# Feed-forward layers by seven block products in place of eight, in a four-layer attention and feed-forward kernel

## The chip, the cores and the metric

The kernel runs on one core of a Trainium2 chip. The metric is the device time of one execution, in microseconds (us). The engines are named as in the profile: PE is the tensor engine and PEld its weight loads, DVE is VectorE, ACT is ScalarE, POOL is GpSimd, and SP issues the DMA transfers. Code and diffs are cuts: several lines of the kernel may stand on one line, and "..." marks what is left out.

## The reference, cut to what matters

There are four layers on 2048 tokens of width 1024: linear attention (A), feed-forward (B), A, B. Each has a layer norm ahead of it and a residual sum behind it.

```python
def _A_ref(x, wqkv, wo):            # 32 heads of 32
    ...
    pq, pk = phi(q), phi(k)         # phi(t) = where(t > 0, t + 1, exp(t)) + 1e-6
    kv  = einsum("bhsd,bhse->bhde", pk, v);  z = sum over s of pk
    o   = einsum(pq, kv) / (einsum(pq, z) + 1e-6)
    return o @ wo
def _B_ref(x, w_gate, w_up, w_down):      # D = 1024, F = 3584
    return ((x @ w_gate) * (x @ w_up)) @ w_down
x = x + _A_ref(_layernorm(x), ...); x = x + _B_ref(_layernorm(x), ...)   # twice
```

## The kernel before

A small planner records each operation with the memory that it reads and writes, and derives the semaphore waits. Each engine has its own list, taken in order.

The feed-forward layer walks 4 blocks of 512 tokens. For each block it makes 28 gate and 28 up chains of eight matmuls (L756), multiplies them, and then runs the down product over 28 tiles (L776):

```python
for m, bank in ((0, b_g), (1, b_u)):
    ... [e.matmul(psb(bank), wgu[:, w, m, k, cc:cc + 128], xnT[:, k, sb * 512:(sb + 1) * 512],
                  start=(k == 0), stop=(k == KT - 1)) for k in range(KT)]          # L756
P.add("act", lambda e: e.copy(gsb[gi], psb(b_g)), ...)                             # L761
P.add("dve", lambda e: e.tensor_tensor(out=hT[:, hs, :], in0=psb(b_u), in1=gsb[gi], op=ALU.mult), ...)
```

In attention, three stretches follow each other: the K and Q projections; the stretch that forms the K·V products; and the output stretch. The division by the denominator ("normalisation" below, `norm`) runs per token tile of 128 tokens. Eleven of the 16 tiles are normalised during the K·V stretch, the other five inside the output stretch, all through one product buffer:

```python
NNORM = 11
def norm(i):
    P.add("dve", ... tensor_tensor(out=pbuf, in0=x_res[:, i, :], in1=zb, op=ALU.mult))   # L588
    ... tensor_reduce(out=den, in_=pbuf ...); + 1e-6; reciprocal                          # DVE
    P.add("pool", ... tensor_tensor(out=asb[b], in0=pbuf, in1=rden (broadcast), op=ALU.mult))  # L597
    P.add("sp", ... dma_start_transpose(xnT[:, :, i * 128:(i + 1) * 128], asb[b]))
...
for i in range(NST):                     # the output stretch
    if na[0] < NST and i % 3 == 0:
        norm(na[0]); na[0] += 1
    nxt.step_t(1); nxt.b1_one()          # layer norm of the next layer: transpose, scale factor
    y_grp(i, 0)                          # 8 matmuls (L714), residual added on DVE (L720)
    nxt.b2_one()                         # layer norm applied, on ACT (L406)
    y_grp(i, 1)                          # 8 matmuls, copied by ACT (L723), added on POOL (L724)
    if i >= 1:
        nxt.start(i - 1)                 # statistics on DVE (L389), 1/sqrt on POOL (L392, L394)
```

## Time and profile before

The median is 1697.24 us (1696.1 to 1698.99, 4 runs). The first view is the head of the page: busy time, share of the span and instruction count of each engine, and then the chain of work that ended last, by line.

```profile
PE 1636.5 (97%) x7577; PEld 740.3 (44%) x7662; DVE 596.8 (35%) x978; ACT 385.7 (23%) x609; POOL 235.2 (14%) x271
...
PE ps L756 46%; PE ps L776 23%; PE ps L569 7%; POOL arena L597 3%; DVE arena L528 2%; DMA arena<-arena 2%; POOL arena L724 1%; PE ps L634 1%; DVE arena L526 1%; DVE arena L389 1%; POOL arena L394 1%; POOL arena L392 1%; ACT arena L406 1%; SPq L600 1%; ACT arena L723 1%
```

PE is the limit: it is nearly always busy, and two lines of the feed-forward layers make up 69% of the chain. The second view holds groups of instructions: line, engine, operation, shapes, count, then total busy us and mean ns of one, then the idle time before them and what ended it.

```profile
L756 PE MATMUL ps<-arena 128*128 128x512 f16 x3584 | 775.1, 379 | 0.0
...
L714 PE MATMUL ps<-arena 128*128 128x512 bf16 x502 | 122.2, 397 | 34.0 <-DVE arena L720 21.0
```

A matmul lasts 379 ns, but matmuls overlap: 775.1 us over 3584 is 216 ns each, and that is the cost of one more. The output stretch (L714) is another matter: PE idles 34 us before its matmuls, waiting for evacuations.

The third view is the table of stretches, cut at the first matmul of each part: start and end, length, busy us (and instructions) of each engine, granted PE clock (1.00 is full rate), DMA share, GB/s. In order: K/Q, K·V, output, feed-forward, and the same again.

```profile
core 0: us, PE busy (x) PEld busy (x) DVE busy (x) ACT busy (x) POOL busy (x), PEclk, DMA share, GB/s
0.00:124.40 124.40, 111.99 (x528) 50.25 (x539) 97.27 (x181) 79.64 (x125) 51.38 (x79) 1.00 0.39 116
124.40:199.20 74.80, 71.20 (x372) 33.99 (x379) 42.10 (x62) 22.55 (x37) 22.33 (x12) 0.98 0.45 103
199.20:277.70 78.50, 60.42 (x253) 24.58 (x257) 49.66 (x90) 22.98 (x29) 39.05 (x45) 0.96 0.49 102
277.70:858.00 580.30, 579.25 (x2670) 262.86 (x2689) 134.48 (x217) 71.23 (x118) 16.69 (x39) 1.00 0.49 137
858.00:961.60 103.60, 103.07 (x472) 46.98 (x481) 75.39 (x123) 72.63 (x118) 39.56 (x34) 1.00 0.30 89
961.60:1034.90 73.30, 69.76 (x373) 33.59 (x379) 42.01 (x62) 22.44 (x37) 22.25 (x12) 1.00 0.39 91
1034.90:1112.20 77.30, 61.40 (x252) 25.30 (x256) 49.65 (x90) 22.99 (x29) 38.98 (x45) 0.93 0.53 115
1112.20:1695.50 583.30, 579.43 (x2669) 262.73 (x2687) 106.23 (x159) 71.24 (x118) 4.93 (x9) 1.00 0.41 118
```

The feed-forward layers are full (PE busy 579 of 580 and 583 us). The two output stretches are not: PE is busy 60 of 78.5 us and 61 of 77.3 us, so they hold 34 us of idle PE between them.

### The profile page before, as it was taken

Reading aid. Unit: us, or ns where it says so; the run is one execution under the profiler, and the core shown is the slowest. Engines: PE = TensorE matmul, PEld = TensorE weight load, DVE = VectorE, ACT = ScalarE, POOL = GpSimd, SP = SyncE. Lnnn points to the kernel's source line nnn. Section 1 sums busy time; section 2 is a strip of 40 time slices with the busy share of each in tenths; the row PEclk is TensorE's granted clock in tenths of the full one; section 3 lists DMA queues with packets and bytes.
Section 4 is the critical chain, followed back from the end, with each engine's and each line's share of the span. In section 5 each row is a group of like instructions: output and inputs, shape, how many; then the busy total and the mean of one; then the engine's idle time right before and its main releaser. Section 6 shows DMA issues by size and latency. Waiting matters only on the chain.

```text
span 1695.5 us, 18381 instructions
## 1 busy us (share of the span) xinstructions
PE 1636.5 (97%) x7577; PEld 740.3 (44%) x7662; DVE 596.8 (35%) x978; ACT 385.7 (23%) x609; POOL 235.2 (14%) x271
## 2 busy tenths in 40 slices
PE   8999978999999999999999998799999999999999
PEld 3444423444444444444444443244444444444444
DVE  6885665112211211221257667641112111211211
ACT  6661323110110011011057523231101101100110
POOL 4442353000000000000033234520000000000000
PEclk9999999999999999999999999999999999999999
DMA  5143635952453355253460146379405513531520
GB/s 199 38 122 76 151 72 119 320 162 61 131 153 101 106 149 149 57 155 112 138 204 1 51 100 148 74 190 282 128 26 157 152 51 108 149 106 46 156 68 22
DMA packets 370692, 203.07 MB, mean 120 GB/s; under 512 B 101168, under 2 KB 351280, under 8 KB 370608
## 3 DMA queue, kind: packets, MB, share of 16 engines
q1 hardware_dynamic: 370608, 201.89, 43.6%
q8 instruction: 61, 1.00, 0.2%
q14 instruction: 23, 0.19, 0.0%
HBM read 165.68 MB, written 12.58 MB: 105 GB/s over the span
## 4 chain that ended last, share of the span: by engine, by line
PE 77%; issue 7%; POOL 7%; DVE 5%; ACT 2%; DMA 2%; SPq 1%; POOLq 0%; ACTq 0%
PE ps L756 46%; PE ps L776 23%; PE ps L569 7%; POOL arena L597 3%; DVE arena L528 2%; DMA arena<-arena 2%; POOL arena L724 1%; PE ps L634 1%; DVE arena L526 1%; DVE arena L389 1%; POOL arena L394 1%; POOL arena L392 1%; ACT arena L406 1%; SPq L600 1%; ACT arena L723 1%
## 5 line engine op out<-in xcount | busy, mean ns | idle before, releaser
L756 PE MATMUL ps<-arena 128*128 128x512 f16 x3584 | 775.1, 379 | 0.0
L756 PEld LDWEIGHTS ps<-arena 128*128 128x128 bf16 x3584 | 350.3, 98 | 423.5 <-ACT arena L761 1.5
L776 PE MATMUL ps<-arena 128*128 128x512 bf16 x1752 | 384.7, 379 | 2.1
L762 DVE TENSOR_TENSOR arena<-ps,arena 128x512 bf16<-128x512 f32 x224 | 155.1, 692 | 595.5 <-PE ps L756 591.3
L761 ACT CAST arena<-ps 128x512 bf16<-128x512 f32 x224 | 131.2, 587 | 907.8 <-PE ps L756 907.8
L776 PEld LDWEIGHTS ps<-arena 128*128 128x128 bf16 x1792 | 175.4, 98 | 211.4
L569 PE MATMUL ps<-arena 128*128 128x512 bf16 x1003 | 224.4, 380 | 6.8 <-DVE arena L528 4.6
L787 DVE TENSOR_TENSOR arena<-ps,arena 128x512 bf16<-128x512 f32 x64 | 44.3, 692 | 318.0 <-PE ps L776 318.0
L714 PE MATMUL ps<-arena 128*128 128x512 bf16 x502 | 122.2, 397 | 34.0 <-DVE arena L720 21.0
L569 PEld LDWEIGHTS ps<-arena 128*128 128x128 f16 x1024 | 99.1, 98 | 127.6 <-DVE arena L528 9.1
L634 PE MATMUL ps<-arena 128*128 128x512 bf16 x499 | 114.1, 379 | 0.6
L524 ACT ACTIVATE arena<-ps 128x512 f32<-128x512 f32 x128 | 76.6, 598 | 120.9 <-PE ps L569 91.6
L392 POOL TENSOR_SCALAR arena<-arena 128x1 f32<-128x1 f32 x64 | 22.0, 343 | 574.4 <-DVE arena L391 574.3
L714 PEld LDWEIGHTS ps<-arena 128*128 128x128 f16 x512 | 49.9, 102 | 105.9 <-DVE arena L720 30.9
L389 DVE BATCH_NORM_STATS2 arena<-arena 128x6 f32<-128x512 bf16 x128 | 88.3, 690 | 9.4 <-DMA arena<-in_A_x_dram 4.3
L581 POOL TENSOR_TENSOR arena<-arena 128x512 f32<-128x512 f32 x60 | 74.9, 1251 | 111.5 <-DVE arena L528 111.5
L528 DVE SCALAR_TENSOR_TENSOR arena<-ps,arena 128x512 bf16<-128x512 f32 x128 | 88.5, 692 | 4.4
L525 ACT ACTIVATE arena<-arena 128x512 f32<-128x512 f32 x128 | 81.0, 633 | 4.1
L597 POOL TENSOR_TENSOR arena<-arena 128x1024 f16<-128x1024 f32 x32 | 61.3, 1915 | 124.6 <-DVE arena L595 114.9
L526 DVE TENSOR_SCALAR arena<-arena 128x512 f32<-128x512 f32 x128 | 66.4, 519 | 33.1 <-ACT arena L525 32.1
L634 PEld LDWEIGHTS ps<-arena 128*128 128x128 f16 x512 | 49.3, 98 | 55.7
L406 ACT ACTIVATE arena<-arena 128x1024 f16<-128x1024 bf16 x32 | 39.8, 1243 | 111.0 <-DVE arena L400 70.1
(41 smaller groups left out, 361.1 us busy)
## 6 DMA issues: line engine op xcount, KB each, us to landing
arena<-in_B_w_gate_dram SPq DMA_DIRECT2D x112, 512.0 KB, 3.8
arena<-in_B_w_up_dram SPq DMA_DIRECT2D x112, 512.0 KB, 4.8
arena<-in_B_w_down_dram SPq DMA_DIRECT2D x14, 1024.0 KB, 10.1
arena<-in_A_wqkv_dram SPq DMA_DIRECT2D x12, 1024.0 KB, 7.9
arena<-in_A_x_dram SPq DMA_DIRECT2D x31, 256.0 KB, 5.3
arena<-in_A_wo_dram SPq DMA_DIRECT2D x4, 1024.0 KB, 5.8
x_scratch<-arena SPq DMA_DIRECT2D x16, 256.0 KB, 2.0
xn_scratch<-arena SPq DMA_DIRECT2D x16, 256.0 KB, 2.4
```

The lines of the kernel that those rows point to most:

```text
L389: P.add("dve", (lambda h: lambda e: e.bn_stats(st[j][:, 6 * h:6 * h + 6], x_res[:, i, (D // 2) * h:(D // 2) * (h + 1)]))(h), rd=r_x(i, (D ...
L525: P.add("act", lambda e: e.activation(etmp[r], etmp[r], AF.Exp, scale=-1.0), rd=er, wr=er)
L526: P.add("dve", lambda e: e.tensor_scalar(out=etmp[r], in0=etmp[r], scalar1=1e-6, scalar2=None, op0=ALU.add), rd=er, wr=er)
L528: P.add("dve", lambda e: e.scalar_tensor_tensor(out=dst_ap, in0=psb(bank), scalar=C1, in1=etmp[r], op0=ALU.add, op1=ALU.max), prd=[bank], ...
L569: return [e.matmul(psb(bank), xnT[:, k, i * 128:(i + 1) * 128], w[:, k, h * 512:(h + 1) * 512], start=(k == 0), stop=(k == KT - 1)) for k ...
L597: P.add("pool", lambda e: e.tensor_tensor(out=asb[b].rearrange("p (h c) -> p h c", c=32), in0=pbuf.rearrange("p (h c) -> p h c", c=32), in ...
L634: return [e.matmul(psb(bank), xr[:, t, j * 128:(j + 1) * 128], pk[:, h, t, :], start=(t == 0), stop=(t == NST - 1)) for t in range(NST)]
L714: return [e.matmul(psb(bank), xnT[:, g, i * 128:(i + 1) * 128], wp[:, g, dh * 512:(dh + 1) * 512], start=(g == 0), stop=(g == NG - 1)) for ...
L756: return [e.matmul(psb(bank), wgu[:, w, m, k, cc:cc + 128], xnT[:, k, sb * 512:(sb + 1) * 512], start=(k == 0), stop=(k == KT - 1)) for k ...
L761: P.add("act", lambda e: e.copy(gsb[gi], psb(b_g)), prd=[b_g], wr=R(O_GS[gi], 1024))
L762: P.add("dve", lambda e: e.tensor_tensor(out=hT[:, hs, :], in0=psb(b_u), in1=gsb[gi], op=ALU.mult), prd=[b_u], rd=R(O_GS[gi], 1024), wr=R( ...
L776: r.append(e.matmul(psb(bank), hT[:, hs, st_ * 128:(st_ + 1) * 128], wd[:, ft, dh * 512:(dh + 1) * 512], start=(ft == 0), stop=(ft == NFT ...
```

## The change

The intent: a product of matrices cut into 2 by 2 blocks can be formed with seven block products and some additions, in place of eight products. The change does this one level deep. Gate and up are cut by contraction half and output half, the tokens in pairs of 512. The kernel now makes two passes of 1024 tokens per layer; a pass has 28 units (gate and up alternating) of seven products of four matmuls, and a down part of seven products. One bank of PSUM (the memory that matmuls write to), X, is a running chain: product 1, then 6, then 7, then 4 are added into it, and ACT copies the partial sum out between them.

```diff
+def unit(ps_, u):                       # one gate or up block: 7 products of 4 matmuls (L878)
+    X, Y, Z = B_GX[u % 2], B_GY[u % 2], B_GZ
+    # 1: a11 b11   2: a12 b21   3: S4 b22   4: a22 T4   5: S1 T1   6: S2 T2   7: S3 T3
+    part1:   pe("1", X, True);  cp(0, X);  pe("2", Z, True);  fin(0, Z, 0)
+    part2:   pe("6", X, False); cp(1, X)                       # cp = ACT copy of the bank (L882)
+    part3:   pe("5", Y, True);  pe("7", X, False); cp(2, X); fin(1, Y, 2)
+    part_p4: pe("4", X, False); fin(2, X, None)                # one unit later
+    part_p3: pe("3", Y, False); fin(3, Y, 1)                   # fin = DVE, bank + copy (L602)
+def prep_s(n):                          # weight sums S1..S4, DVE, 16-bit (L599); first pass only
+    tt(sv[:, 0], a21, a22, ALU.add); tt(sv[:, 1], sv[:, 0], a11, ALU.subtract); ...
+def wd_tick(ph):                        # sums of the down weights, spread over the first pass
+    if ph == 0: wd_load(j)
+    elif ph == 1: wd_prep(j); wd_store(j); wdn[0] += 1
 ...
+cur[0](); prev[1](); cur[2](); prev[3](); ring_issue(); cur[4]()
+if jit: store_s(n); prep_s(n + 2)       # jit = first pass of the first feed-forward layer
+ticks(u)                                # layer norm steps, down-weight sums
```

The weight sums go to DRAM as they are made and are streamed back in the three later passes. Sums of activations (T1 to T4) and of the hidden blocks are made on DVE too. The activation and the hidden operands are fp16.

The same diff also touches attention:

```diff
-    NNORM = 11
+    NNORM = 14
-    pbuf = vf(O_P, D)
+    pbufs = [vf(o, D) for o in O_P]     # O_P = [O_ZACC, RE], used as pbufs[i % 2]
-    if na[0] < NST and i % 3 == 0:
+    if na[0] < NST:
         norm(...)
     nxt.step_t(1); nxt.b1_one()
+    if i >= 2:
+        nxt.start(i - 2)
     y_grp(i, 0); nxt.b2_one(); y_grp(i, 1)
-    if i >= 1:
-        nxt.start(i - 1)
```

Besides, the second attention layer takes its tokens in the order in which the new down part finishes them. PSUM banks and SBUF places are reassigned.

## The prediction

> **What bounds the kernel now.** The tensor engine. The page has PE busy 97% of 1695.5 us at a granted clock of 0.994. In the chain of waits, the gate/up line (L756) and the down line (L776) hold 46% and 23%. The table of stretches gives the two feed-forward layers 582 and 585 us, PE busy 581 in each; they run 5376 matmuls of 512 columns at 216 ns (775.1 us over 3584). PE idles mainly in the attention output stretches (204 to 276 us: busy 53.5 of 71.6; 1042 to 1110: 52.7 of 68.5). There the waits view has PE waiting for evacuations (L720, L723), which sit behind the normalisation chain: one product buffer, 5.1 us a step.
>
> **Removed.** One matmul in eight: 5376 becomes 4704. 672 x 0.216 = 145 us, all on the critical path. Operand types should not change the rate: fp16 activations with bf16 weights already run at 216 ns.
>
> **Added, mostly off the path.**
> - VectorE: 536 PSUM evacuations at 0.692 us (L762's duration) for 288; about 336 SBUF additions or products of 512 16-bit elements, 64 of 1792, 16 of 2048. The trace has no such operation. [...]
> - ScalarE: 392 PSUM copies at 0.59 us for 224, about +100 us.
> - A gate and up pair costs PE 56 x 0.216 = 12.1 us; [...]ScalarE 4.1. A copy has two or three products (0.86 us each) to finish. Hidden.
> - Exception: the first pass of the first feed-forward layer, where the weight sums are made[...]. [...]two of the down-weight preparations are queued directly behind their own load. I expect PE to wait there about 16 us (10 to 35), little in later passes.
> - DMA grows from 202 to about 250 MB. The heaviest stretch asks about 275 GB/s; a slice of the present page moves 320 GB/s without PE waiting.
> - Starts of passes and layers, longer lead into the first pass: +8 us.
>
> **Moved.** The normalisation gets two product buffers and 14 tokens (was 11) during the previous stretch, so the output stretches should shrink from 72 and 68 to about 60 us: -20 us.
>
> **Sum.** 1697 - 145 + 16 + 8 - 20 is about 1556 us. Range 1532 to 1595. Faster by over 2%: 0.96; within 2%: 0.03; slower: 0.01.
>
> **What would show it right or wrong.** Matmul groups: 3136 gate/up and 1568 down matmuls, 216 ns each by busy time over count. Stretches: feed-forward layers near 530 (first) and 512 us (second), PE busy about 508 in each; PE's missing time concentrated in the first layer's first pass, released by VectorE. [...] Attention output stretches near 60 us each.
>
> **What would make it wrong.** [...]VectorE held up in order behind loads or layer norm, so that PE stalls on PSUM banks in every pass; the single bank for the second product turning into a per-unit wait; no gain in the attention stretches (1575 us).

The sum came to about 1556 us: 1697 - 145 + 16 + 8 - 20. The 16 us, and the 8 us for starts, are estimates.

## The result, and the profile after

The changed kernel takes 1547.34 us (1544.87 to 1547.89, 4 runs). The ratio to the kernel before is 0.9113, with a 95% interval of 0.9097 to 0.9129. Ratios here are the mean time of one kernel's fast runs over that of the other's fast runs of the same rounds, so they differ a little from the ratio of the medians. All outputs are right. The head of the page after, and its groups:

```profile
PE 1492.5 (97%) x6925; PEld 674.1 (44%) x6990; DVE 967.5 (63%) x1642; ACT 503.3 (33%) x793; POOL 246.6 (16%) x271
```

```profile
L878 PE MATMUL ps<-arena 128*128 128x512 f16 x3136 | 685.4, 381 | 17.5 <-ACT arena L882 12.3 <-DVE arena L602 5.2
...
L882 ACT ACTIVATE arena<-ps 128x512 f32<-128x512 f32 x336 | 200.4, 596 | 551.4 <-PE ps L878 550.6 <-DVE arena L602 0.8
...
L599 DVE TENSOR_TENSOR arena<-arena 128x512 f16<-128x512 bf16 x140 | 53.1, 419 | 10.4 <-DMA arena<-in_B_w_down_dram 9.9
...
L599 DVE TENSOR_TENSOR arena<-arena 128x2048 f16<-128x2048 f16 x16 | 19.5, 1216 | 0.0
```

PE is as full as before, with less to do. The 16-bit additions of 512 elements take 419 ns where a bf16 pair is written as fp16 (x140, above), and 429 ns where all is fp16 (x196). DVE has 371 us more work. The table of stretches after, in the same order:

```profile
0.00:124.10 124.10, 111.77 (x529) 50.02 (x540) 97.28 (x181) 79.48 (x125) 51.48 (x79) 1.00 0.40 117
124.10:198.30 74.20, 71.21 (x372) 34.04 (x379) 56.48 (x74) 22.31 (x37) 37.35 (x15) 0.98 0.51 114
198.30:256.00 57.70, 55.28 (x252) 24.84 (x256) 46.56 (x91) 24.86 (x30) 31.99 (x45) 1.00 0.56 116
256.00:784.20 528.20, 514.10 (x2343) 230.04 (x2352) 328.91 (x605) 131.39 (x210) 11.10 (x27) 0.99 0.67 205
784.20:901.00 116.80, 107.07 (x472) 47.41 (x480) 79.03 (x139) 77.31 (x124) 42.50 (x43) 0.97 0.40 116
901.00:972.90 71.90, 69.54 (x371) 33.61 (x378) 55.61 (x73) 22.19 (x37) 37.36 (x15) 1.00 0.56 121
972.90:1030.70 57.80, 55.38 (x253) 24.88 (x256) 45.35 (x88) 25.01 (x31) 32.02 (x45) 1.00 0.66 162
1030.70:1546.20 515.50, 508.14 (x2343) 229.28 (x2351) 258.28 (x397) 120.77 (x200) 2.74 (x5) 1.00 0.53 164
```

Line by line against the table before, the two feed-forward layers give 52.1 and 67.8 us, together 119.9. The two output stretches give 20.8 and 19.5, together 40.3. The K·V stretches give 2.0, the first K/Q stretch 0.3. The second K/Q stretch **costs** 13.2 us. The sum is 149.3, the difference of the two spans (1695.5 and 1546.2).

Two things stand out: over a quarter of the gain (40.3 of 149.3 us) comes from the output stretches of attention, and one stretch got worse. A third shows when the feed-forward layers are cut into passes. These are the four gate/up passes:

```profile
256.00:445.20 189.20, 176.27 (x786) 77.01 (x786) 142.37 (x314) 62.26 (x102) 2.96 (x5) 0.97 0.75 237
...
529.60:699.80 170.20, 169.50 (x785) 76.50 (x785) 95.86 (x171) 66.66 (x106) 6.33 (x16) 1.00 0.74 207
...
1030.70:1204.10 173.40, 170.09 (x786) 76.32 (x786) 87.15 (x148) 62.25 (x102) 2.74 (x5) 1.00 0.56 167
...
1288.50:1458.80 170.30, 169.56 (x786) 76.57 (x786) 84.54 (x140) 58.51 (x98) 0.00 (x0) 1.00 0.58 177
```

784 matmuls at 216 ns are 169.3 us. Three passes are within about 4 us of that; the first loses 20. DVE is busy only 142 of its 189 us, so DVE is not full there. What PE waited for in the first pass stands at the end of its group:

```profile
L878 PE MATMUL ps<-arena 128*128 128x512 f16 x784 | 176.2, 387 | 12.9 <-ACT arena L882 7.7 <-DVE arena L602 5.2
```

### The profile page after: what moved, and what is told of

The parts are those of the page before. It is cut to its first block, busy times and chain, and to the rows that moved or that the text cites. A ratio compares the mean times of both kernels' runs of the same rounds, so it can differ in the third digit from the quotient of the medians.

```text
span 1546.2 us, 18008 instructions
## 1 busy us (share of the span) xinstructions
PE 1492.5 (97%) x6925; PEld 674.1 (44%) x6990; DVE 967.5 (63%) x1642; ACT 503.3 (33%) x793; POOL 246.6 (16%) x271
## 4 chain that ended last, share of the span: by engine, by line
PE 79%; DVE 11%; issue 4%; ACT 3%; POOL 2%; DMA 1%; SPq 0%; DVEq 0%; POOLq 0%; ACTq 0%
PE ps L878 41%; PE ps L988 22%; PE ps L807 6%; PE ps L661 5%; PE ps L727 4%; DVE arena L550 3%; DVE arena L548 2%; DVE arena L408 1%; DVE arena L681 1%; DVE arena L684 1%; DMA arena<-in_B_w_down_dram 1%; DVE arena L599 1%; ACT arena L425 1%; POOL arena L413 1%; ACT arena L882 1%
## 5 line engine op out<-in xcount | busy, mean ns | idle before, releaser
L878 PE MATMUL ps<-arena 128*128 128x512 f16 x3136 | 685.4, 381 | 17.5 <-ACT arena L882 12.3
L602 DVE SCALAR_TENSOR_TENSOR arena<-ps,arena 128x512 f16<-128x512 f32 (+2 forms) x536 | 365.0, 689 | 437.3 <-PE ps L988 160.8
L878 PEld LDWEIGHTS ps<-arena 128*128 128x128 f16 (+1 forms) x3136 | 306.0, 98 | 396.3 <-ACT arena L882 21.4
L882 ACT ACTIVATE arena<-ps 128x512 f32<-128x512 f32 x336 | 200.4, 596 | 551.4 <-PE ps L878 550.6
L988 PE MATMUL ps<-arena 128*128 128x512 f16 (+1 forms) x1548 | 337.4, 379 | 1.1
L661 PE MATMUL ps<-arena 128*128 128x512 bf16 x1003 | 228.3, 384 | 16.0 <-DVE arena L550 13.9
L988 PEld LDWEIGHTS ps<-arena 128*128 128x128 f16 x1568 | 153.4, 98 | 185.0
L599 DVE TENSOR_TENSOR arena<-arena 128x512 f16<-128x512 f16 (+3 forms) x416 | 222.6, 556 | 17.0 <-DMA arena<-in_B_w_down_dram 9.9
L661 PEld LDWEIGHTS ps<-arena 128*128 128x128 f16 x1024 | 99.6, 99 | 140.3 <-DVE arena L550 20.3
L807 PE MATMUL ps<-arena 128*128 128x512 bf16 x502 | 111.0, 379 | 4.8 <-DVE arena L813 3.9
L727 PE MATMUL ps<-arena 128*128 128x512 bf16 x499 | 114.2, 379 | 0.6
L425 ACT ACTIVATE arena<-arena 128x1024 f16<-128x1024 bf16 x48 | 59.5, 1239 | 132.2 <-DVE arena L419 119.7
L546 ACT ACTIVATE arena<-ps 128x512 f32<-128x512 f32 x128 | 76.0, 594 | 64.3 <-PE ps L661 37.9
L690 POOL TENSOR_TENSOR arena<-arena 128x1024 f16<-128x1024 f32 x32 | 80.0, 2499 | 89.2 <-DVE arena L688 88.0
L807 PEld LDWEIGHTS ps<-arena 128*128 128x128 f16 x512 | 49.8, 98 | 65.8 <-DVE arena L813 4.9
L727 PEld LDWEIGHTS ps<-arena 128*128 128x128 f16 x512 | 49.2, 98 | 55.7
```

What stands on the lines that cost most here:

```text
L599: P.add("dve", lambda e: e.tensor_tensor(out=out, in0=a, in1=b, op=op), rd=rd, wr=wr, prd=prd)
L602: P.add("dve", lambda e: e.scalar_tensor_tensor(out=out, in0=a, scalar=sc, in1=b, op0=ALU.mult, op1=op1), rd=rd, wr=wr, prd=prd)
L661: return [e.matmul(psb(bank), xnT[:, k, i * 128:(i + 1) * 128], w[:, k, h * 512:(h + 1) * 512], start=(k == 0), stop=(k == KT - 1)) for k ...
L727: return [e.matmul(psb(bank), xr[:, t, j * 128:(j + 1) * 128], pk[:, h, t, :], start=(t == 0), stop=(t == NST - 1)) for t in range(NST)]
L807: return [e.matmul(psb(bank), xnT[:, g, i * 128:(i + 1) * 128], wp[:, g, dh * 512:(dh + 1) * 512], start=(g == 0), stop=(g == NG - 1)) for ...
L878: P.add("pe", lambda e: [e.matmul(psb(bank), w[:, k, :], x[:, k, :], start=(start and k == 0), stop=(k == 3), skip_group_check=True) for k ...
```

## The experiments

Ten kernels were run, in three groups. Each group shares its runs of the kernel before, whose medians were 1697.21, 1697.49 and 1696.31 us. The changed kernel was not run again in them, so a difference from its 1547.34 us is one between groups.

### Why the first pass loses 20 us, and the second K/Q stretch 13 us

The PE timeline at the start of the first pass shows the pattern (start, length, instructions; in brackets the idle time before and what ended it):

```profile
256.02 7.07 PE L878 MATMUL ps<-arena 128*128 128x512 f16 x32
265.26 7.90 PE L878 MATMUL ps<-arena 128*128 128x512 f16 x28 [2.17 <-ACT arena L882]
275.79 7.90 PE L878 MATMUL ps<-arena 128*128 128x512 f16 x28 [2.63 <-ACT arena L882]
285.86 4.67 PE L878 MATMUL ps<-arena 128*128 128x512 f16 x13 [2.17 <-ACT arena L882]
```

PE stops three times for an ACT copy. And the 28 matmuls after the first two stops take 7.9 us each, where the same 28 take 6.2 us in run `e2_wd_early` below at full rate: the records of the granted clock show a half-rate period of 3.41 us after each of the three stops (the first from about 266.4 us). So each of the first two costs its idle time and, on top, 1.7 us (7.9 less 6.2); for the third, with as long a period, the same is our estimate. The 12.9 us of idle and three times 1.7 us make 18 of the 20 us. The chain that ended last says what the copy waited for:

```profile
272.76 1.10 DVE arena L599 x3
273.86 0.14 DVE arena L419
274.02 1.24 ACT arena L425
275.26 0.49 ACT arena L882
275.79 5.33 PE ps L878 x16
```

Read upwards: PE waits for a 0.6 us copy (L882); the copy stands behind a layer norm application on ACT (L425, 1.24 us); that waits for a scale factor of 0.2 us on DVE (L419); and that stands behind the weight sums (L599). Later in the pass, three stops have another cause:

```profile
311.11 5.64 DMA arena<-in_B_w_down_dram
...
316.77 0.44 DVE arena L599
...
318.33 0.61 DVE arena L602
318.99 29.54 PE ps L878 x136
```

Here a sum of down weights waits on DVE for its own load, issued just before it, and the evacuation for which PE waits (L602) stands behind. These three stops (2.50, 0.80 and 1.93 us) were not followed by half rate: the granted clock stayed at 1.00 from 290.3 us to the end of the pass. In the second K/Q stretch the chain runs in a ring of 9.9 us per token tile, and again L419 and L425 are links of it:

```profile
851.73 0.70 DVE arena L408
...
853.06 0.58 POOL arena L413
...
853.66 0.23 DVE arena L419
853.91 1.24 ACT arena L425
855.15 0.49 ACT arena L546
```

L546 is the first step of the K/Q evacuation. The rival to all this "in-order" theory: these stretches simply hold more work than DVE and ACT can do, and its order does not matter. Three single edits tell the two apart, each alone, and then all together.

**Layer norms of the second K/Q stretch on DVE, as before the change.**

```diff
     lnp.on_act = False
+    if not is_last:
+        nxt.on_act = False
```

> The changed kernel, with the layer norms of the second K/Q stretch (784 to 901 us, 116.8 us) applied on VectorE as the kernel before does, not on ScalarE. Theory A: PE stalls there because the ScalarE normalisation (1.24 us, L425) waits in order for a VectorE statistic and holds back the K/Q evacuation on ScalarE; taking it off ScalarE brings the stretch to 104 to 109 us and the time down by 8 to 13 us. Rival B: the stretch is longer because five more tokens are normalised inside it at all (statistics and normalisation work moved in from the feed-forward layer); then the engine that does it matters little and the stretch stays within 3 us of 116.8.

Measured: 1537.96 us (1535.62 to 1540.43, 4 runs), ratio 0.906. The stretch fell to 105.6 us. ACT no longer waits for L419 at all, and DVE has more work in the stretch than it had (81.0 us against 79.0), ACT 4 us less (73.4 against 77.3). Neither more tokens in the stretch nor the work on DVE was therefore what made it long; the ACT link was. Theory A holds. The 2 us that remain against the kernel before (103.6) were not followed up.

**Down-weight loads issued one block ahead.**

```diff
-if ph == 0 and j < NJ: wd_load(j)
-elif ph == 1 and j < NJ: wd_prep(j); wd_store(j); wdn[0] += 1
+if ph == 0 and j == 0: wd_load(0)
+elif ph == 1 and j < NJ:
+    wd_prep(j); wd_store(j)
+    if j + 1 < NJ: wd_load(j + 1)
+    wdn[0] += 1
```

> The changed kernel, with each down-weight load issued directly after the sums of the block before it, so that a load never has its own sums queued right behind it. Theory A: the three stops of PE at 311, 353 and 387 us in the first pass of the first feed-forward layer (three waits of VectorE for that load, 5.3 to 5.8 us each in the chain, 9.9 us of VectorE idle in all) go; the first pass falls from 188.9 us by 4 to 10 us and the total by as much. Rival B: VectorE is simply full in that pass (142 us busy of 189, but little room left per unit), so the work is only moved and the pass changes by less than 2 us.

Measured: 1541.74 us (1540.7 to 1543.2, 4 runs), ratio 0.9083. The first pass fell from 189.2 to 183.7 us. VectorE still waits for the load, but 5.0 us in place of 9.9, at most 1.8 us at a time, and PE waits for L602 once, 1.5 us, in place of three times, 5.2 us. Theory A holds, at the lower end, and not all of the 5.5 us is the loads': the first stop of the pass, again of 2.17 us, was this time not followed by half rate (the 28 matmuls after it took 6.22 us, against 7.90), which is worth 1.7 us.

**The layer norm application always uses a scale factor made a unit earlier.**

```diff
 self.step_t(1)
-if self.q_n: self.b2_one(); self.b1_one()
-else:        self.b1_one(); self.b2_one()
+self.b2_one(); self.b1_one()
```

> The changed kernel, where a unit's ScalarE normalisation always uses a statistic made a unit earlier (one order of two calls changed). Theory A: the stalls in the first three or four units of the first pass (256 to 290 us: 33 us for about 20.9 us of matmuls, granted clock 0.80 to 0.85) come from ScalarE, which stands in order behind that statistic, which stands in order behind four weight sums on VectorE; the stalls go, the first pass shrinks by 7 to 12 us, the second layer's first pass by 1 to 3 us. Rival B: VectorE's load of weight sums and statistics itself is too much in these units, and the stalls stay within 3 us of what they are.

Measured: 1533.67 us (1531.41 to 1537.28, 5 runs), ratio 0.9041. The first pass fell to 180.4 us and the second layer's first pass from 173.4 to 170.3. The first 37 us of the pass now ran at a granted clock of 1.00 where the changed kernel had 0.85 in its first 34 us. No work was removed; two calls changed places. Theory A holds. The execution profiled is the fastest of the five, and 3.0 us of its gain lie in the first K·V stretch (71.2 us against 74.2), which the edit doesn't touch: there a stop that was 2.57 us is 1.21 us, and the four matmuls after it take 1.04 us, where they took 1.89.

**All three.**

> All three edits in one kernel. If the three are separate causes their gains add: about 1547 less 25 to 30 us, near 1520 us. If the stalls hide each other (VectorE full in the first pass), the sum falls short of the parts by over 5 us.

Measured: 1520.92 us (1520.22 to 1521.05, 4 runs), ratio 0.8959 to the kernel before. The three gains by medians, 9.4, 5.6 and 13.7 us, add to 28.7; together they give 26.4. So they are nearly separate causes, as far as such sums can tell: the mean granted clock of the executions profiled was 0.993 in the changed kernel, 0.993, 0.994 and 0.998 with one edit each, and 0.999 with all three, so fewer half-rate periods are part of the last two gains. This is the fastest kernel. Its first pass and its second K/Q stretch:

```profile
256.20:432.50 176.30, 170.63 (x785) 75.95 (x785) 141.94 (x314) 62.36 (x102) 2.95 (x5) 1.00 0.84 254
...
771.60:877.20 105.60, 103.78 (x472) 46.57 (x480) 80.94 (x139) 73.35 (x119) 42.24 (x43) 1.00 0.43 120
```

DVE does the same 142 us of work in this pass as before the repair, in 13 us less time. That settles that the pass was not short of DVE throughput. Seven of its 176 us are still above the matmuls' own 169.3.

### Where the 40 us in the output stretches come from

The diff changes three things there: two product buffers, 14 tiles normalised ahead, and the layer norm statistics of a tile started one tile later. It also uses other PSUM banks. The first three were put one after another into the kernel **before**, with no block product anywhere.

**Two buffers and 14 tiles ahead** (`NNORM = 14`, `pbufs[i % 2]`, `norm` at every step of the output stretch until all are done):

> The kernel before, with nothing of the seven products: only two product buffers for the attention normalisation, and 14 of its 16 tokens done in the stretch ahead (was 11). Theory A: this alone is what shortens the attention output stretches from 71.6 and 68.5 us to about 52; the kernel before gains 28 to 36 us, to 1661 to 1669 us. Rival B: the later start of the layer norms in that stretch, their other order and the other PSUM banks do it, and this part alone gains under 12 us.

Measured: 1669.64 us (1668.17 to 1670.04, 4 runs), ratio 0.9838. The output stretches fell from 78.5 and 77.3 to 65.7 us each. The gain of 27.9 us is just short of what theory A said, and the stretches did not reach the 57.8 us of the changed kernel. So it is most of the cause, not all.

The product on GpSimd itself became longer: 1915 ns on average with one buffer in the kernel before, where VectorE waits for it (39.3 us in all), and 2471 ns with two. In the changed kernel, also with two, it takes 2499 ns on average: 26 of the 32 overlap VectorE's product of a later tile (L681) and take 2634 ns on average, the other six 1913 ns. The overlap still paid.

**14 tiles ahead, one buffer** (the same without `pbufs`):

> The kernel before with 14 tokens normalised ahead, but still one product buffer. If the buffer matters (each token 5.1 us in series, 14 of them 71 us, more than the stretch ahead leaves), the tail spills into the output stretch and less than two thirds of the gain of the run with two buffers is there. If only the place of the norms matters, the gain is within 4 us of that run.

Measured: 1705.32 us (1705.2 to 1705.45, 4 runs), ratio 1.005: slower than the kernel before. The output stretch is again short (64.8 us), but the K·V stretch ahead of it grew from 74.8 to 91.2 us at a mean granted clock of 0.89, and PE sits idle there, 18.0 us in one stop. The expectation had the loss in the output stretch; it came one stretch earlier:

```profile
124.80:216.00 91.20, 72.71 (x379) 34.23 (x378) 50.99 (x74) 22.49 (x37) 27.95 (x15) 0.89 0.44 105
```

One buffer forces 5.1 us per tile (in the chain, L597 on POOL every 5.1 us). The placement alone is worth nothing; it needs the buffer.

**The changed kernel with one buffer** (`O_P = [O_ZACC, O_ZACC]`):

> The changed kernel with one product buffer. If the second buffer matters, attention loses 6 to 20 us over its two layers; if only the place of the norms matters, under 4 us.

Measured: 1582.03 us (1581.73 to 1583.27, 4 runs), ratio 0.9322, 34.7 us slower than with two. The K·V stretches are 90.5 and 91.4 us, against 74.2 and 71.9. The direction was right, the size was not. PE stops once for 18.0 us in each of the two stretches:

```profile
207.06 1.89 PE L767 MATMUL ps<-arena 128*128 128x512 bf16 x4 [17.97 <-DVE arena L744]
```

L744 closes the K·V products and stands on DVE behind the last of the 14 normalisations, 13 of which wait 2 us for the buffer; the changed kernel's stop there is 2.6 us in the first stretch. The mean granted clock of the first of these stretches is 0.91, against 0.98 in the changed kernel, but PE is busy 72.0 us in it, against 71.2: from these two figures we estimate that its half rate adds about 1 us more to the matmuls than there. So the expectation had the backlog itself too small.

**Two buffers, 14 ahead, and the statistics one tile later**, again in the kernel before:

```diff
 nxt.b1_one()
+if i >= 2:
+    nxt.start(i - 2)
 y_grp(i, 0); nxt.b2_one(); y_grp(i, 1)
-if i >= 1:
-    nxt.start(i - 1)
```

> The kernel before with two product buffers, 14 tokens ahead, and besides the layer norm statistics of a token taken one token later and issued ahead of the residual additions, as the changed kernel has them. The run without this last edit left the output stretches at 65.7 us each, the changed kernel has 57.8. Theory: there VectorE stands in order behind the residual addition of GpSimd on the token just before; a token of distance lets it run, both stretches come to 57 to 60 us and the total to 1651 to 1659 us. Rival: the other PSUM banks of the changed kernel do it; then the stretches stay at 64 us or more.

Measured: 1654.68 us (1654.33 to 1656.12, 4 runs), ratio 0.9755. Both output stretches are at 57.8 us, like the changed kernel's, with the old PSUM banks; the banks had no part in it. First without this edit, then with it, each in two views: the output stretch in the table of stretches, and what VectorE waited for in it (total us, times, longest).

```profile
197.50:263.20 65.70, 57.65 (x257) 23.88 (x256) 38.95 (x80) 22.92 (x30) 29.84 (x42) 1.00 0.45 94
```

```profile
DVE arena L401 <- POOL arena L395: 22.9, 13, 2.7
```

```profile
198.40:256.10 57.70, 55.53 (x257) 24.82 (x256) 42.03 (x83) 24.88 (x30) 31.84 (x45) 1.00 0.54 109
```

```profile
DVE arena L401 <- POOL arena L395: 6.0, 12, 2.1
```

In these kernels these line numbers are one higher than in the kernel before. L395 is the 0.6 us power on POOL, queued behind the 1.16 us residual addition of the tile just before; L401 on DVE waits for it, and the next residual addition on DVE, for which PE waits, stands behind L401. Without the edit a tile's scale factor (L401) is asked for right after its statistics, but for a normalisation that may be due; with it, a residual addition on DVE comes between. That distance takes most of the wait away. So the attention part alone is worth 41.6 us in the kernel before.

**The changed kernel with the normalisation as before** (one buffer, 11 ahead, every third step; the later statistics stay):

> The changed kernel with the normalisation of attention as before: one product buffer, 11 tokens ahead and the other five in every third place of the output stretch; the later statistics stay. What the sevenths alone bring is then left, with the slower K/Q stretch: if the attention part is worth the 27 us that it brought alone in the kernel before, this run is at 1566 to 1578 us; if the later statistics already repair most of the output stretch, at 1552 to 1562 us.

Measured: 1576.67 us (1574.31 to 1579.81, 4 runs), ratio 0.9289, 29.3 us slower than the changed kernel. Only about 13 us of it lie in the output stretches (63.6 and 65.2 us). Some 15 us lie in the gate/up first passes, 196.0 and 181.9 us, against 189.2 and 173.4. One execution was cut up this way. Its groups show five layer norm applications on ACT in each of these passes, in place of three, and PE's waits for ACT copies there are 10.6 and 9.2 us; that the layer norms spill into these passes fits this, but was not tested by itself. The edit also issues two weight loads later in the output stretch; PE is not seen waiting for a load.

### Is the new ACT work hidden?

```diff
-P.add("act", lambda e: e.activation(tm[i][0], psb(bank), AF.Copy, scale=SG), ...)
+for _ in range(2):
+    P.add("act", lambda e: e.activation(tm[i][0], psb(bank), AF.Copy, scale=SG), ...)
```

> The changed kernel with every ScalarE copy of a partial sum in the feed-forward layers done twice, so that each takes about 1.2 us in place of 0.6, and ScalarE is busy 200 us more. Theory A: the copies are hidden behind two or three products of other banks; the three later passes stay within 2 us each of 170 us and the total grows by under 10 us, nearly all of it in the first pass. Rival B: the evacuation of the shared accumulation bank sets PE's pace in every unit: 0.6 us more on each of 336 copies that PE waits for, 60 us or more in all.

Measured: 1581.71 us (1577.48 to 1583.25, 4 runs), ratio 0.9317, 34.4 us slower. Both expectations failed as stated. The four gate/up passes went from 189.2, 170.2, 173.4 and 170.3 to 202.3, 181.6, 182.7 and 172.5 us. Only the last pass, the one without layer norms, stayed near what theory A said. Cutting the second pass into six pieces shows where its 11 us went (three of the six):

```profile
543.10:573.00 29.90, 27.04 (x123) 11.46 (x122) 17.56 (x35) 18.61 (x31) 2.87 (x8) 1.00 0.80 242
...
603.00:633.00 30.00, 28.06 (x130) 12.12 (x127) 13.42 (x24) 19.49 (x32) 0.00 (x0) 1.00 0.74 203
633.00:663.00 30.00, 30.00 (x141) 13.23 (x140) 14.56 (x25) 18.84 (x34) 0.00 (x0) 1.00 0.60 175
...
```

PE issues 123, 120 and 130 matmuls in the first three pieces, and 141 from 633 us on. By the groups of those pieces ACT applies layer norms (L425) six times in the first 60 us, twice in the third piece, and never after it; and PE stops eight times for 0.97 us, each stop ending 1.2 us, one doubled copy, after an application. ACT is busy about 18 to 20 of 30 us throughout. So ACT is never full, and a doubled copy alone (1.2 us) is hidden behind two or three other products. It is no longer hidden where a layer norm application of 1.24 us can stand in front of it. There the changed kernel has less to spare than the doubling adds, 0.6 us on each of the three copies of a unit.

## Why the prediction was right or wrong, point by point

The predicted time was 1556 us and the measured one 1547.34, inside the range, and the direction was right. The sum is close partly by luck, because two errors nearly cancel.

- **"672 x 0.216 = 145 us, all on the critical path": right.** The feed-forward layers were expected near 530 and 512 us and measured 528.2 and 515.5. Their gain of 119.9 us is the 145 us less 20 in the first pass, 4 in the second layer's first pass, and small remainders. The prediction had 24 us there, 16 for the first pass and 8 for starts; the loss is 25, but the 8 us of starts were not measured by themselves.
- **The 16-bit additions on VectorE: measured only afterwards.** The kernel before has no such operation. The trace of the changed kernel has 1216 ns for 2048 elements, 1081 for 1792, and for 512 elements 429 in fp16 and 419 where a bf16 pair is written as fp16.
- **VectorE as the limit of the first pass: the step that failed inside a right number.** The loss in the first pass was predicted at 16 us (10 to 35) and is 20. The prediction had VectorE fuller than PE in that pass, an author's estimate. But DVE was busy 142 of 189 us; it was not full. Adding up durations overstates such a load, since instructions overlap in part: the 139 mixed additions of this pass, 419 ns each, are busy 52.7 us, not 58. PE was released there by ACT copies (7.7 us) more than by DVE (5.2 us), where the prediction had VectorE. The causes were two kinds of wait in the engines' lists and the half clock after three of the stops. The prediction named one of them ("two of the down-weight preparations are queued directly behind their own load") and missed the other, the ACT layer norm behind DVE's sums. The run with all three edits recovered 13 of the 20 us without less work.
- **"Hidden" for the new ACT copies: right in the outcome, with less slack than it sounded.** The doubled copy showed it: slack in units without layer norm, next to none in units with it.
- **"The output stretches should shrink from 72 and 68 to about 60 us: -20 us": the term that was mis-sized.** With the same cuts they measured 52.2 each, 35.8 us less; cut at first matmuls, 40.3 us less. The mechanism that it named (two buffers, 14 tiles) brought 27.9 us when run alone in the kernel before. The rest came from starting the statistics one tile later, which the prediction did not mention.
- **Not predicted: the second K/Q stretch, +13.2 us.** The prediction took the rest of attention as unchanged. The flag that puts layer norms on ACT stayed set into the next layer; the run with it cleared got 11.2 us of that back. This error and the one above have opposite signs, 13 against 16 to 20 us, which is why the total looks better than its parts.
- **DMA was not the limit: right in volume, incomplete in kind.** 254 MB moved (203 before; predicted about 250). No PE stop was traced to a lack of bandwidth, but three to loads issued just before their sums.

Whether half rate follows a stop could not be told in advance here. Stops of 2.17, 2.63 and 2.17 us were each followed by 3.41 us at half rate in the changed kernel, and the stop of 2.50 us (316.5 to 319.0 us) was not. The first stop of the pass was 2.17 us in the runs `e2_wd_early` and `e7_after_one_buf` too, and the 28 matmuls after it took 6.22 us there, against 7.90. So the length of a stop alone does not tell; what decides was not shown.

## What to carry to other kernels

When PE is full and a change trades matmuls for vector work, price the matmuls at their spacing (216 ns here), and then look less at how busy the other engines become than at what stands in front of each evacuation in their lists: a 0.2 us scale factor there stopped PE for over 2 us (2.17 to 2.63), and the half rate after it, where it came, cost 1.7 us more; late loads stopped it for 0.8 to 2.5 us. Split a measured gain by stretches before crediting it: here 41.6 us were to be had without the block products (which leaves about 107 us for them), from two buffers, an earlier normalisation and statistics one tile later, and the placement alone made things worse until the buffer came with it. Then look for the stretch that got slower; its repair, with two other edits of order, was worth a further 26 us.
